# A gather of attention weights in two column halves: an mLSTM with a gated feed-forward layer on one core

## The chip, the cores and the metric

The kernel runs on one core of one Trainium2 chip. The metric is the device time of one launch in microseconds; the lower the better. Of the kernel before there are three timed runs and one profiled execution, which gives the span from the first to the last instruction of the program.

## The reference, cut to what matters

For each of 4 batches and 8 heads, 768 tokens run through a gated recurrence, and its output goes through a gated feed-forward layer:

```
for t in range(S):                                   # S = 768, head size D = 40
    m_new = maximum(f_gate[t] + m, i_gate[t])
    f_stab, i_stab = exp(f_gate[t] + m - m_new), exp(i_gate[t] - m_new)
    C = f_stab * C + i_stab * outer(v[t], k[t])      # 40 x 40 per batch and head
    n = f_stab * n + i_stab * k[t]
    y[t] = sigmoid(o_gate[t]) * (C @ q[t]) / maximum(abs(n @ q[t]), 1)
x = y as 3072 tokens x 320
out = (sigmoid(x @ w_gate) * (x @ w_val)) @ w_out     # 320 -> 1536 -> 320
```

All inputs and the output are float32.

## The kernel before, in words

The recurrence is computed in chunks: 768 tokens are 6 chunks of 128, and with 4 batches that makes 24 *units* (chunk c, batch b), each with 128 tokens and all 8 heads. Within a unit the work is attention-like. The state of the earlier chunks comes in as a separate product.

The stages of a unit, with the names that stand in the profile:

- **a** (`st_a`): q and k are transposed on TensorE (tile `pt`, L357 and L373).
- **b** (`st_b`): the scores of each head, keys on the output's 128 partitions and queries along its columns (tile `s`, L426 in chunks 0 and 1, L434 later), are multiplied on VectorE by the decay matrix (`d`, L427 and L435). The result stays in `d`: 128 keys x 8 heads x 128 queries.
- **c** (`st_c`): the *gather*. For each head one matmul has the 128 x 128 block of `d` as the stationary operand and the head's 128 x 41 values (`v`, with a column of ones for the denominator) as the moving operand: 128 queries x 41 into the PSUM tile `av` (L452). Before it stands the part from the state (`in`, L447). VectorE adds the two (L454) and divides. `st_e` then updates the state (`cs`, L500).
- **d** (`st_d`): the unit's output is transposed (`xt`, L488) into the feed-forward layer's operands `xh` and `xl`.

Around these stages runs the feed-forward layer. `ffn_up` makes, for a tile of 128 hidden columns and 256 or 512 tokens, the gate and value products (`pg`, L532, L534, L537); `ffn_down` multiplies by the output weights (`po`, L554 to L556). Its operands are split in a high and a low part, so each product is made of three matmuls. This layer is most of TensorE's work.

The first two units (0,0) and (0,1) are done in `opening()`, in an order written out by ranks; their gather is a function of its own (L697). Everything after is emitted in the order of a table of positions, and a scheduler then orders each engine's instructions by priority: by default an instruction's place in the program, raised where a piece of code is wrapped in `tc.high_priority(offset=...)`. Stages a to d are wrapped in that with an offset of 1 (`HPO`), weights with 2 (`WPO`). Where instructions of equal standing are ready together, the scheduler mixes them, so a gather's matmuls can stand among those of `pg` or `po`.

Of the kernel before, what the change touches and what calls it, by code (L numbers as in the profile page):

```python
# [67 lines left out]
    },  # L68
    'unpin': [],
}  # L70
GROUPS = ((0, 3), (3, 3), (6, 2))

# [2 lines left out]
def mlstm_then_gated_ffn_kernel(  # L75
# [13 lines left out]
    nc = tc.nc  # L89
    B, H, S, D = q.shape  # L90
    P = 128
# [30 lines left out]
    qt, kt, vt, ot = {}, {}, {}, {}  # L122
# [18 lines left out]
    dm = {}  # L141

    def dm_tile(c, b):
        dm[(c, b)] = big.tile([P, H, L], F32, tag="dmat", name=f"d_{c}_{b}", bufs=3)
        return dm[(c, b)]
# [193 lines left out]
    def bank(c, b, shape, name):  # L339
        return ps_a.tile(shape, F32, tag="pa", name=f"{name}_{c}_{b}")  # L340
# [51 lines left out]
    def stack():  # L392
# [6 lines left out]
        for x, dst, i in ((1, ks, 0), (0, qs, 1)):  # L399
# [4 lines left out]
            nc.sync.dma_start(dst[one].rearrange("p (m g) t -> p m (g t)", m=3).bitcast(F32),  # L404
                              sc[:, 0, :, x, :].rearrange("m d w -> d m w"))

    dlast = {}

    def d_last(u):
# [29 lines left out]
    def st_c(c, b):  # L439
        u = (c, b)  # L440
        nc.scalar.activation(ot[u], ot[u], AF.Tanh, scale=0.5)
        t1 = None
        if c > 0:
            pi = bank(c, b, [P, H, DA], "in")
            for g, (h0, nh) in enumerate(GROUPS):
                r = nh * D
                nc.tensor.matmul(pi[:, h0 : h0 + nh, :], qk[u][:r, g, :], cst[:r, b, g, : nh * DA], start=True, stop=True)  # L447
            t1 = two.tile([P, H, DA], F32, tag="t1", name=f"t1_{c}_{b}")
            nc.vector.tensor_tensor(t1, pi, dec[:, c, b * H : (b + 1) * H].unsqueeze(2).broadcast_to([P, H, DA]), ALU.mult)
        pv = bank(c, b, [P, H, DA], "av")  # L450
        for h in range(H):
            nc.tensor.matmul(pv[:, h, :], dm[u][:, h, :], vt[u][:, h, :], start=True, stop=True)  # L452
        if c > 0:
            nc.vector.tensor_tensor(t1, t1, pv, ALU.add)  # L454
            hs = t1
        else:
            hs = pv
        halfden(u, hs)
        times_den(u)
# [4 lines left out]
    def halfden(u, hs):  # L464
        c, b = u
        den = two.tile([P, H], F32, tag="den", name=f"den_{c}_{b}")
        nc.vector.tensor_scalar(den, hs[:, :, D], -2.0, 2.0, ALU.mult, ALU.max)
        nc.vector.scalar_tensor_tensor(den, hs[:, :, D], 2.0, den, ALU.mult, ALU.max)
        nc.vector.reciprocal(den, den)
        rden[u] = den  # L470
        nc.vector.scalar_tensor_tensor(ot[u], ot[u], 1.0, hs[:, :, :D], ALU.add, ALU.mult)

    def times_den(u):
        c, b = u
        xin[u] = x = two.tile([P, 3 * P], F32, tag="x", name=f"x_{c}_{b}", bufs=1)
        eng = E('ro0' if c == 0 and b < 2 else 'ro')
        eng.tensor_tensor(x[:, :DM].rearrange("p (h d) -> p h d", d=D), ot[u],
                          rden[u].unsqueeze(2).broadcast_to([P, H, D]), ALU.mult)
        E('xd0' if c == 0 and b < 2 else 'xd').tensor_copy(x[:, DM:], x[:, 2 * P : DM])
# [94 lines left out]
    def opening():  # L574
        us = ((0, 0), (0, 1))
# [48 lines left out]
        d = [dm_tile(0, b) for b in range(2)]  # L624
# [5 lines left out]
        pmb, pt, ps, pv, pc, px, sp = {}, {}, {}, {}, {}, {}, {}  # L630
# [5 lines left out]
        def ptile(tag, shape, name):  # L636
            return (ps_a if tag == "pa" else ps_o).tile(shape, F32, tag=tag, name=name)
# [56 lines left out]
        def gather(b):  # L694
            pv[b] = p = ptile(tags["v", b], [P, H, DA], f"av_0_{b}")
            for h in range(H):
                nc.tensor.matmul(p[:, h, :], d[b][:, h, :], vt[us[b]][:, h, :], start=True, stop=True)  # L697

        def ogate(b):
            nc.scalar.activation(ot[us[b]], ot[us[b]], AF.Tanh, scale=0.5)  # L700
# [7 lines left out]
        w = {x: None for x in ((0, 0), (1, 0), (2, 0))}  # L708
# [25 lines left out]
        for b in range(2):  # L734
            for n in range(2):
                op(f"sp{b}{n}", spread, (b, n))
                op(f"ex{b}{n}", expd, (b, n), f"sp{b}{n}")
                op(f"mk{b}{n}", mask, (b, n), f"ex{b}{n}")
            op(f"dl{b}", d_last, (us[b],), f"mk{b}0", f"mk{b}1")
            for g in range(3):  # L740
                op(f"tr{b}{g}", trans, (b, g))
                op(f"cp{b}{g}", copy, (b, g), f"tr{b}{g}")
                op(f"qb{b}{g}", qbd, (b, g), f"cp{b}{g}")
                op(f"sc{b}{g}", score, (b, g), f"qb{b}{g}")
                op(f"ti{b}{g}", times, (b, g), f"sc{b}{g}", f"dl{b}")
            op(f"kw{b}", kweight, (b,), f"dl{b}", *(f"tr{b}{g}" for g in range(3)))
            op(f"og{b}", ogate, (b,))
            op(f"ga{b}", gather, (b,), *(f"ti{b}{g}" for g in range(3)))
            op(f"na{b}", norm_a, (b,), f"ga{b}", f"og{b}")
            op(f"nb{b}", norm_b, (b,), f"na{b}")  # L750
            op(f"xt{b}", st_d, us[b], f"nb{b}")
# [33 lines left out]
    start = [0.0]  # L785
# [9 lines left out]
    for u in range(2, NU):  # L795
        for st in "abcde":
            c, b = divmod(u, B)
# [16 lines left out]
    for u in reversed(range(2, NU)):  # L814
# [5 lines left out]
        n = u + (1 if u == B * (PARAM['V32'] + 1) - 1 else 2)  # L820
# [19 lines left out]
    for u in range(2, NU):  # L840
        c, b = divmod(u, B)
# [18 lines left out]
    def emit(p, kind, kk):  # L860
# [7 lines left out]
        elif kind == "w":  # L868
            with tc.high_priority(offset=PARAM["WPO"]):
                w_next(wseq[kk])  # L870
        elif kind == "g":
            if kk == 0:
                dmat_load(1, 0)
            else:
                gates_of(2, NCH)
        elif kind == "h":
            gate_transpose(ag, at, *((1, 2), (2, NCH))[kk], None)
        elif kind == "k":
            gates_turn(*((1, 2), (2, NCH))[kk])
        elif kind == "e":  # L880
            if last is None:
                dmat(c, b)
            else:
                with tc.issue_after(last.ins):
                    dmat(c, b)
        else:
            with tc.high_priority(offset=PARAM["HPO"]):
                if kind == "a":
                    st_a(c, b)
                elif kind == "b":  # L890
                    st_b(c, b)
                elif kind == "c":
                    st_c(c, b)
                    st_e(c, b)
                    prefetch(c + 1, b)
                else:
                    st_d(c, b)
# [45 lines left out]
```

## Time and profile before

| | |
|---|---|
| Timed runs, median (lowest to highest) | 572.12 us (571.66 to 572.26) |
| Span of the profiled execution | 569.9 us |
| TensorE matmul records, share of the span busy | 96% |
| TensorE weight loads, share of the span busy | 87% |
| VectorE, ScalarE, GpSimd busy | 56%, 41%, 28% |
| Gather, weight loads busy (22 units, L452) | 46.8 us |
| Granted TensorE clock, mean of the span | 0.988 |

The page gives the profiled execution's span and no other time of it; the median of the runs is 2.2 us longer. PE is TensorE's matmuls and PEld its weight loads, which are recorded apart. A float32 matmul in the program shows as two pairs of a weight load and a matmul, so one unit's gather is 16 pairs. Records of neighbouring matmuls overlap, and so their lengths don't add up; the distance from one start to the next does. In a record's shape the first pair of numbers is rows*columns of the stationary operand and the second the shape of what the record names.

### The profile page before, as it was taken

Reading aid. Unit: us, or ns where it says so; the run is one execution under the profiler, and the core shown is the slowest. Engines: PE = TensorE matmul, PEld = TensorE weight load, DVE = VectorE, ACT = ScalarE, POOL = GpSimd, SP = SyncE. Lnnn points to the kernel's source line nnn. Section 1 sums busy time; section 2 is a strip of 40 time slices with the busy share of each in tenths; the row PEclk is TensorE's granted clock in tenths of the full one; section 3 lists DMA queues with packets and bytes.
Section 4 is the critical chain, followed back from the end, with each engine's and each line's share of the span. In section 5 each row is a group of like instructions: output and inputs, shape, how many; then the busy total and the mean of one; then the engine's idle time right before and its main releaser. Section 6 shows DMA issues by size and latency. Waiting matters only on the chain.

```text
span 569.9 us, 9906 instructions
## 1 busy us (share of the span) xinstructions
PE 546.7 (96%) x3587; PEld 497.0 (87%) x3587; DVE 319.5 (56%) x739; ACT 232.2 (41%) x581; POOL 162.2 (28%) x231
## 2 busy tenths in 40 slices
PE   8667999999999999999999999999999999999997
PEld 7565988788899999998888888888888888999996
DVE  5788878895755645555555544545543545432322
ACT  5285657754443442352243241433342332232322
POOL 5567646575420241311322310332210210000000
PEclk9789999999999999999999999999999999999999
DMA  9797747242674947354666544685644824010000
GB/s 197 193 240 185 202 123 192 93 115 54 169 173 119 183 103 182 100 147 125 167 125 156 132 141 129 149 171 124 140 125 134 206 56 121 4 47 2 24 2 23
DMA packets 131641, 72.27 MB, mean 127 GB/s; under 512 B 103113, under 2 KB 120777, under 8 KB 131593
## 3 DMA queue, kind: packets, MB, share of 16 engines
q1 hardware_dynamic: 130504, 71.39, 50.6%
q8 instruction: 28, 0.46, 0.3%
q10 hardware_dynamic: 1088, 0.26, 0.2%
q14 instruction: 21, 0.16, 0.1%
HBM read 56.95 MB, written 14.68 MB: 126 GB/s over the span
## 4 chain that ended last, share of the span: by engine, by line
PE 85%; DVE 7%; ACT 3%; issue 2%; POOL 2%; POOLq 0%; DVEq 0%; ACTq 0%
PE pg L532 34%; PE po L554 7%; PE po L556 7%; PE po L555 7%; PE av L452 6%; PE pg L534 6%; PE pg L537 6%; PE in L447 2%; PE s L434 2%; PE pt L373 2%; PE xt L488 2%; PE cs L500 2%; PE s L426 1%; DVE dc L264 1%; ACT d L226 1%
## 5 line engine op out<-in xcount | busy, mean ns | idle before, releaser
L539 ACT ACTIVATE sg<-pg 128x256 f32<-128x256 f32 (+1 forms) x103 | 48.3, 469 | 174.3 <-PE pg L537 174.2
L540 DVE SCALAR_TENSOR_TENSOR sg<-sg,pg 128x256 f32<-128x256 f32 (+1 forms) x103 | 53.9, 524 | 113.9 <-ACT sg L539 110.6
L532 PE MATMUL pg<-xh,wl 128*128 128x256 f32 (+1 forms) x412 | 111.1, 342 | 1.2 <-POOL wl L304 1.2
L532 PE MATMUL pg<-xh,wh 128*128 128x256 f32 (+1 forms) x412 | 110.9, 343 | 0.4 <-DVE sg L540 0.4
L532 PE MATMUL pg<-xl,wh 128*128 128x256 f32 (+1 forms) x412 | 108.7, 339 | 0.0
L556 PE MATMUL po<-oh,gl 128*128 128x320 f32 x288 | 93.0, 323 | 0.0
L554 PE MATMUL po<-oh,gh 128*128 128x320 f32 x288 | 92.3, 321 | 0.4 <-ACT gh L543 0.4
L555 PE MATMUL po<-ol,gh 128*128 128x320 f32 x288 | 92.4, 321 | 0.0
L544 DVE TENSOR_TENSOR gl<-sg,gh 128x256 fp32r<-128x256 f32 (+1 forms) x103 | 59.6, 579 | 35.5 <-ACT gh L543 34.9
L532 PEld LDWEIGHTS pg<-xh,wl 128*128 128x128 f32 x412 | 70.9, 191 | 8.5 <-POOL wl L304 1.4
L532 PEld LDWEIGHTS pg<-xh,wh 128*128 128x128 f32 x412 | 70.9, 191 | 5.8 <-DVE sg L540 0.6
L532 PEld LDWEIGHTS pg<-xl,wh 128*128 128x128 f32 x412 | 69.3, 190 | 6.6
L543 ACT ACTIVATE gh<-sg 128x256 fp32r<-128x256 f32 (+1 forms) x103 | 51.7, 502 | 47.7 <-DVE sg L540 47.7
L554 PEld LDWEIGHTS po<-oh,gh 128*128 128x128 f32 x288 | 54.5, 189 | 2.0 <-ACT gh L543 0.6
L555 PEld LDWEIGHTS po<-ol,gh 128*128 128x128 f32 x288 | 54.4, 189 | 1.3
L556 PEld LDWEIGHTS po<-oh,gl 128*128 128x128 f32 x288 | 54.2, 188 | 0.5 <-DVE gl L544 0.2
L534 PE MATMUL pg<-xh,w 128*128 128x256 f32 (+1 forms) x206 | 52.9, 332 | 0.7 <-POOL v L139 0.4
L537 PE MATMUL pg<-xl,w 128*128 128x256 f32 (+1 forms) x206 | 53.1, 331 | 0.0
L452 PEld LDWEIGHTS av<-v,d 128*128 128x128 f32 x352 | 46.8, 191 | 2.2 <-DVE d L427 0.6
L452 PE MATMUL av<-v,d 128*128 128x41 f32 x352 | 45.5, 269 | 0.4 <-DVE d L427 0.3
L508 POOL TENSOR_TENSOR cst<-cst,cdec 120x246 f32<-120x246 f32 (+1 forms) x32 | 16.0, 519 | 98.9 <-PE in L447 98.9
L235 POOL TENSOR_SCALAR_AFFINE_SELECT d<-d 128x1024 f32<-128x1024 f32 x22 | 24.2, 1101 | 50.1 <-ACT d L230 46.0
(128 smaller groups left out, 834.5 us busy)
## 6 DMA issues: line engine op xcount, KB each, us to landing
d<-mscr SPq DMA_DIRECT2D x22, 512.0 KB
ks<-scr SPq DMA_DIRECT2D x16, 360.0 KB
qs<-scr SPq DMA_DIRECT2D x16, 360.0 KB
k<-in_k_dram SPq DMA_DIRECT2D x24, 160.0 KB
v<-in_v_dram SPq DMA_DIRECT2D x24, 160.0 KB
o<-in_o_gate_dram SPq DMA_DIRECT2D x24, 160.0 KB
st_o<-in_moe_w_out_dram SPq DMA_DIRECT2D x12, 320.0 KB
out_dram<-ob SPq DMA_DIRECT2D x24, 160.0 KB
```

The lines of the kernel that those rows point to most:

```text
L235: nc.gpsimd.affine_select(out=d, in_=d, pattern=[[0, H], [1, L]], compare_op=ALU.is_ge, fill=0.0, base=0, channel_multiplier=-1)
L452: nc.tensor.matmul(pv[:, h, :], dm[u][:, h, :], vt[u][:, h, :], start=True, stop=True)
L532: nc.tensor.matmul(pg[n], w[n][:, a, fs], x[c][:, a, n0:n1], start=(i + a == 0), stop=False)
L534: nc.tensor.matmul(pg[n], w2[n][:, fs], xh[c][:, 2, n0:n1], start=False, stop=False)
L537: nc.tensor.matmul(pg[n], w2[n][:, fs], xl[c][:, 2, n0:n1], start=False, stop=True)
L539: nc.scalar.activation(sg, pg[0], AF.Tanh, scale=0.5)
L540: nc.vector.scalar_tensor_tensor(sg, sg, 1.0, pg[1], ALU.add, ALU.mult)
L543: last = nc.scalar.activation(gh[u][:, :nt], sg, AF.Copy)
L544: E('gl0' if c == 0 else 'gl').tensor_tensor(gl[u][:, :nt], sg, gh[u][:, :nt].bitcast(F32), ALU.subtract)
L554: nc.tensor.matmul(po[t], g1[:, ts], oh[:, j, :], start=(j == 0), stop=False)
L555: nc.tensor.matmul(po[t], g1[:, ts], ol[:, j, :], start=False, stop=False)
L556: nc.tensor.matmul(po[t], g0[:, ts], oh[:, j, :], start=False, stop=(j == NF - 1))
```

## The change

Each head's gather is made of two matmuls in place of one. The first has the 64 stationary columns of the first 64 queries and writes partitions 0 to 63 of `av`, the second has the other 64 columns and writes partitions 64 to 127. The moving operand is the same 128 x 41 for both. This holds in all 24 units, the opening's too, by a new function `by_columns`. In `st_c` the gather is also wrapped in a priority with an offset of 20. The entries `SC` and `SPO` are not read.

```
+    'AV': 2,
+    'SC': 1,
+    'APO': 20,
+    'SPO': 20,
...
+    def by_columns(dst, lhs, rhs, n):
+        w = P // n
+        for x in range(n):
+            xs = slice(x * w, (x + 1) * w)
+            nc.tensor.matmul(dst[xs], lhs[:, xs], rhs, start=True, stop=True)
...
         pv = bank(c, b, [P, H, DA], "av")
-        for h in range(H):
-            nc.tensor.matmul(pv[:, h, :], dm[u][:, h, :], vt[u][:, h, :], start=True, stop=True)
+        with tc.high_priority(offset=PARAM['APO']):
+            for h in range(H):
+                by_columns(pv[:, h, :], dm[u][:, h, :], vt[u][:, h, :], PARAM['AV'])
...
         def gather(b):
             pv[b] = p = ptile(tags["v", b], [P, H, DA], f"av_0_{b}")
             for h in range(H):
-                nc.tensor.matmul(p[:, h, :], d[b][:, h, :], vt[us[b]][:, h, :], start=True, stop=True)
+                by_columns(p[:, h, :], d[b][:, h, :], vt[us[b]][:, h, :], PARAM['AV'])
```

Line numbers move by 10 or 11: the gather's matmuls all stand at L415 (in `by_columns`), `in` at L457, `cs` at L511, `pg` at L543 and following, `po` at L565 to L567.

How PE's order moves. First, unit (1,0) before, where its gather begins; the numbers in a name are chunk and batch (`av_1_0`), and in `pg0_0_5_0` the half, the chunk, the hidden tile and the first token tile:

```order
L555 MATMUL po3_0_915<-ol_105,gh_0_3_2_1001 128x320
L452 MATMUL av_1_0_1055<-v_1_0_397,d_1_0_451 128x41
L556 MATMUL po3_0_915<-oh_104,gl_0_3_2_1002 128x320
L452 MATMUL av_1_0_1055<-v_1_0_397,d_1_0_451 128x41
L532 MATMUL pg0_0_5_0_1105<-xh_0_343,wh0_98 128x512
L452 MATMUL av_1_0_1055<-v_1_0_397,d_1_0_451 128x41
L532 MATMUL pg0_0_5_0_1105<-xh_0_343,wh0_98 128x512
```

The same place on PE in the changed kernel:

```order
L566 MATMUL po3_0_947<-ol_105,gh_0_3_2_1033 128x320
L415 MATMUL av_1_0_1087<-v_1_0_413,d_1_0_467 64x41 x16
L567 MATMUL po3_0_947<-oh_104,gl_0_3_2_1034 128x320
L543 MATMUL pg0_0_5_0_1145<-xh_0_359,wh0_98 128x512 x2
L543 MATMUL pg0_0_5_0_1145<-xh_0_359,wl0_99 128x512 x2
```

The heads no longer stand apart with a wider matmul between each two; sixteen half-width matmuls stand in one row.

Second, unit (1,1) on PE before, at the end of its part from the state:

```order
L532 MATMUL pg0_0_9_0_1443<-xh_0_343,wh0_98 128x512
L447 MATMUL in_1_1_1383<-cst_106,qk_1_1_1136 128x123
L532 MATMUL pg0_0_9_0_1443<-xh_0_343,wl0_99 128x512
L447 MATMUL in_1_1_1383<-cst_106,qk_1_1_1136 128x82
L532 MATMUL pg0_0_9_0_1443<-xh_0_343,wl0_99 128x512
L452 MATMUL av_1_1_1389<-v_1_1_556,d_1_1_563 128x41
L532 MATMUL pg0_0_9_0_1443<-xl_0_344,wh0_98 128x512
L452 MATMUL av_1_1_1389<-v_1_1_556,d_1_1_563 128x41
```

And in the changed kernel:

```order
L457 MATMUL in_1_1_1423<-cst_106,qk_1_1_1176 128x123
L415 MATMUL av_1_1_1429<-v_1_1_580,d_1_1_587 64x41 x16
L543 MATMUL pg0_0_9_0_1491<-xh_0_359,wh0_98 128x512
L457 MATMUL in_1_1_1423<-cst_106,qk_1_1_1176 128x123
L543 MATMUL pg0_0_9_0_1491<-xh_0_359,wl0_99 128x512
L457 MATMUL in_1_1_1423<-cst_106,qk_1_1_1176 128x82
```

Here the gather has moved ahead of the last two matmuls of `in`, which VectorE reads first, and the matmuls of `pg` follow it whole.

## The prediction

> **What bounds the kernel now.** I read the head of the page first: how busy each engine is, then the chain of work that ended last, then the costliest groups.
>
> ```profile
> span 569.9 us, 9906 instructions
> PE 546.7 (96%) x3587; PEld 497.0 (87%) x3587; DVE 319.5 (56%) x739; ACT 232.2 (41%) x581; POOL 162.2 (28%) x231
> ...
> PE 85%; DVE 7%; ACT 3%; issue 2%; POOL 2%; POOLq 0%; DVEq 0%; ACTq 0%
> PE pg L532 34%; PE po L554 7%; PE po L556 7%; PE po L555 7%; PE av L452 6%; PE pg L534 6%; PE pg L537 6%; PE in L447 2%; PE s L434 2%; PE pt L373 2%; PE xt L488 2%; PE cs L500 2%; PE s L426 1%; DVE dc L264 1%; ACT d L226 1%
> ...
> L452 PEld LDWEIGHTS av<-v,d 128*128 128x128 f32 x352 | 46.8, 191 | 2.2 <-DVE d L427 0.6
> L452 PE MATMUL av<-v,d 128*128 128x41 f32 x352 | 45.5, 269 | 0.4 <-DVE d L427 0.3
> ```
>
> TensorE (PE) is the bound: 85% of the last chain, and the gather (L452) alone 6% of it. Each float32 product shows as two records, each a weight load and a matmul: 22 units x 8 heads x 2 = 352. The other 32 are the opening's (L697). Next, busy time by stretch, from the first unit after the opening to the last up-projection:
>
> ```profile
> 57.00:556.00 499.00, 495.28 (x3291) 452.00 (x3290) 273.15 (x639) 196.71 (x481) 127.47 (x172) 1.00 0.48 121
> ```
>
> Columns: length, then PE, weight loads, DVE, ACT and POOL. PE works 495.28 of 499.00 us at the full granted clock (1.00). PE time saved or added here goes to the end almost one for one, and a shift on another engine costs nothing while PE has this backlog.
>
> What sets a gather's length is in the timeline of the weight loads:
>
> ```profile
> 50.01 1.86 PEld L452 LDWEIGHTS av<-v,d 128*128 128x128 f32 x16 [0.24 <-ACT qk L361]
> 51.79 0.68 PEld L500 LDWEIGHTS cs<-v,k 128*120 128x120 f32 x6
> ```
>
> Sixteen loads from 50.01 until the next line's at 51.79: 1.78 us, 0.111 us each. A load lasts 0.191 us and its matmul 0.269 us, both more than that step, so they overlap, and the step is the weight loads': moving only 41 columns takes less (below, 82 columns step at 0.07). Does a gather hide among wider matmuls? Unit (1,0) answers:
>
> ```profile
> 85.12 0.43 PEld L452 LDWEIGHTS av<-v,d 128*128 128x128 f32 x2
> 85.47 0.19 PEld L532 LDWEIGHTS pg<-xh,wl 128*128 128x128 f32 x1
> 85.58 0.43 PEld L452 LDWEIGHTS av<-v,d 128*128 128x128 f32 x2
> ...
> 308.49 0.63 PE L532 MATMUL pg<-xh,wl 128*128 128x512 f32 x2
> 308.96 0.63 PE L532 MATMUL pg<-xl,wh 128*128 128x512 f32 x2
> ```
>
> One head plus one 512-wide pg takes 0.46 us (85.12 to 85.58). A pg alone takes 0.235 (0.47 for two). The head still costs 0.225, its two loads. So standing together or scattered, a unit's gather costs 1.78 us: 22 x 1.78 = 39.2 us here.
>
> **The change, part by part.** (1) Priority. The order shows each gather as one block (once 15+1), where six units were broken up by wider matmuls and five more had one head apart. By the row above that alone is worth nothing. In some units it also stands a few matmuls earlier; what could be late is DVE's product of scores and weights. DVE stands idle 23.1 us waiting for gathers, and the loads of L452 waited for that product 0.6 us in all (its row above); I take 0.
>
> ```profile
> DVE t L454 <- PE av L452: 23.1, 18, 2.4
> ```
>
> The order of loads, memsets and stores on SP and POOL shifts by a few places with it; DMA share is 0.48 in this stretch, so 0. If that cover were gone, one late transfer would show as a PE wait of a microsecond or so.
>
> (2) Twice as many loads, half as wide: 32 records a unit instead of 16. A narrower load is cheaper, by the two shapes of the state update (window just behind the gather above):
>
> ```profile
> L500 PEld LDWEIGHTS cs<-v,k 128*120 128x120 f32 x4 | 0.5, 184 | 0.0
> L452 PEld LDWEIGHTS av<-v,d 128*128 128x128 f32 x2 | 0.3, 192 | 0.0
> L500 PEld LDWEIGHTS cs<-v,k 128*80 128x80 f32 x2 | 0.3, 150 | 0.1
> ```
>
> (192 - 150) / 48 columns = 0.875 ns a column, so 64 columns fewer take 56 ns off the 111 ns step: 55 to 56 ns for one load.
>
> (3) A narrow tile. The trace has one kind of load that uses only a strip of the array, the gate transposes (32 rows, form 32*128). Around them PE pauses:
>
> ```profile
> 90.20 0.30 PE L500 MATMUL cs<-v,k 128*80 128x82 f32 x2
> 90.43 0.43 PE L195 MATMUL ptg<-ident,gin 32*128 32x32 f32 x4
> 90.79 0.41 PE L554 MATMUL po<-oh,gh 128*128 128x320 f32 x1
> 91.05 0.31 PE L555 MATMUL po<-ol,gh 128*128 128x320 f32 x1
> ...
> 90.43 0.32 PEld L195 LDWEIGHTS ptg<-ident,gin 32*128 32x128 f32 x4
> ...
> L500 PE MATMUL cs<-v,k 128*80 128x82 f32 x2 | 0.3, 234 | 0.0
> ...
> 306.85 0.31 PE L555 MATMUL po<-ol,gh 128*128 128x320 f32 x1
> 307.00 0.31 PE L556 MATMUL po<-oh,gl 128*128 128x320 f32 x1
> ```
>
> The two cs matmuls last 0.234 and end at 90.50, so the second started at 90.27, 0.07 after the first; without a pause the next would start at 90.34. The four ptg loads step at (0.32 - 0.137) / 3 = 0.06. The second po comes 0.26 after the first where 0.15 is usual, so the block really ended at 91.05 - 0.15 = 90.90. That is 0.56 us for 0.24 us of loads: 0.32 us for entering and leaving, the exposed first load of the next line included. (The 0.137 is the mean of these four:)
>
> ```profile
> L195 PEld LDWEIGHTS ptg<-ident,gin 32*128 32x128 f32 x4 | 0.3, 137 | 0.1
> ```
>
> Bounds for a gather in halves: 0 (the 80-column cs shows no pause) to 0.32. A half that must land on output partitions 64 to 127 is a strip of the array, like ptg, so I take 0.32. The Trainium skill ("TensorEngine Tiling (Array Packing)", Key Properties) says that changing the tiling mode drains TensorE; this trace agrees at ptg, with the 0.32 us above.
>
> (4) Whether the two halves load at once. No row shows two loads into different columns. Bounds: 32 steps a unit (one at a time) or 16 (in pairs). The nearest row speaks for one at a time:
>
> ```profile
> 65.44 0.12 PEld L357 LDWEIGHTS pt<-ident,q 128*80 128x80 f32 x1 [0.30 <-DVE cdec L213]
> 65.45 0.23 PEld L532 LDWEIGHTS pg<-xh,wl 128*128 128x128 f32 x1
> 65.62 0.12 PEld L357 LDWEIGHTS pt<-ident,k 128*80 128x80 f32 x1
> 65.72 0.19 PEld L532 LDWEIGHTS pg<-xh,wl 128*128 128x128 f32 x1
> ```
>
> The load issued at 65.45 right behind another takes 0.23 instead of 0.19: it queues. But those two fill the same columns. The halves of a head fill disjoint columns and write disjoint partitions, and the cost per column in (2) is a cost of pushing columns in, which two separate strips need not share. I take pairs, at ptg's 0.06 a step (0.056 by proportion is its lower end): 16 x 0.06 = 0.96, + 0.32 = 1.28 us a unit, 0.50 less than 1.78. The same skill page and section says that different tiles can load and multiply in parallel, which would be this case; no run here shows it yet.
>
> (5) The opening. The last chain and the loads:
>
> ```profile
> 14.25:28.50 14.25, 9.15 (x50) 7.82 (x49) 10.10 (x22) 4.04 (x11) 7.19 (x9) 0.72 0.74 194
> ...
> 20.15 3.41 PE av L697 x16
> 23.56 0.47 PE xt L488 x2
> ...
> 20.15 3.26 PEld L697 LDWEIGHTS av<-v,d 128*128 128x128 f32 x16 [2.79 <-DVE d L689]
> 23.15 0.69 PEld L488 LDWEIGHTS xt<-ident,x 128*128 128x128 f32 x3
> ```
>
> The second opening gather lies on the chain and takes 23.15 - 20.15 = 3.00 us, 1.69 times a usual one, in a stretch whose granted clock is 0.72. Scaled, it saves 0.50 x 1.69 = 0.85. The first is followed by a DVE wait until 20.15, so 0.
>
> Sum: 22 x 0.50 + 0.85 = 11.85 us off a span of 569.9. The median of the runs, 572.12, is 2.2 us over that span (start and end around it), and I leave those as they are: 572.1 - 11.9 = **560.3 us**. With 0.056 steps a unit is 1.22, giving 559.
>
> **The rivals.** *One load at a time* (slower). The mechanism is at the weight loads of L452: if halves queue like the rows at 65.45, a unit takes 32 x 0.056 = 1.79 + 0.32 = 2.11, or 2.24 at 0.06. That is 0.33 to 0.46 more in 22 units and 0.6 to 0.8 in the opening: +7.9 to +10.9, 580 to 583 us. It decides once a pair of halves takes longer than (1.78 - 0.32) / 16 = 0.091 us. For it: every close pair of loads in this trace queues. Against it: none of them are to different columns. The Trainium skill ("TensorE: Matmul & The Clock Gate", The mechanism) says a weight load overlaps matmuls in flight only where the row group differs, and here both halves use all rows; but L452's loads, all of one row group, already start while matmuls of 0.269 us are in flight, so the trace does not bear that rule out as it stands.
>
> *Half overlap.* If records keep their order (two loads of one half, then two of the other), only neighbouring loads of different halves may pair: three steps a head, 24 x 0.06 = 1.44 + 0.32 = 1.76. That is 0.02 less: 571.6, no change.
>
> *No pause.* If the halves cost no entry and exit (as the 80-column cs), with pairs: 0.96 a unit, 0.82 x 22 + 1.4 = 19.4 off: 552.7.
>
> **How the numbers follow.** Pairs with a pause 0.59 (own range 555 to 566), no pause 0.04, half overlap 0.10, one at a time 0.27. This kernel's measurement tells 0.2%, 1.1 us, from no change. Half overlap spreads around zero by some 2 us, as the pause may be 0.1 us off per unit: 0.04 of it faster, 0.04 same, 0.02 slower. Faster 0.59 + 0.04 + 0.04 = 0.67, same 0.04, slower 0.27 + 0.02 = 0.29. The range goes from 554, just above the case without pause, to 582, which takes in about half of one at a time; some 0.17 is left out.
>
> **What would show it.** Right: the gather's loads in the timeline at 32 a unit, with two starts per 0.06 us and some 1.0 us from first to last; PE busy time in the stretch down by some 10 us; before the first and behind the last a gap of 0.1 to 0.2 us; 5 to 6% of the chain in L452 (now L415) becoming 4 to 5%. Wrong: loads stepping at 0.055 to 0.065 each (one at a time), a block of 1.4 us (half overlap), or a gather that starts without a gap. Were waits of the gather for DVE to reach 0.2 us a unit, part (1) would be wrong by 5 us.

## The result, and the profile after

The changed kernel takes 577.71 us (median of 4 runs, 574.92 to 578.26) beside 571.89 us for the kernel before in the same session: ratio 1.0102, 95% interval [1.0073, 1.0131]. It is slower by 1.0%; 560.3 us had been forecast. Among the experiments below, one execution of e10 (the profiled one, 733 us at a granted clock of 0.65 throughout) and one of e4 (625.8 us) are left out of the ratios. The changed kernel's profiled execution took 577.27 us, with this page (head, the chain of waits by engine and by line) and, from the groups kept apart by shape, these rows of the gather:

```profile
span 575.6 us, 10660 instructions
PE 541.6 (94%) x3971; PEld 484.0 (84%) x3971; DVE 329.9 (57%) x739; ACT 231.5 (40%) x581; POOL 159.5 (28%) x231
...
PE 79%; DVE 8%; POOL 4%; ACT 4%; issue 3%; DMA 2%; SPq 0%; POOLq 0%; DVEq 0%; ACTq 0%
PE pg L543 32%; PE po L567 7%; PE po L565 6%; PE po L566 6%; PE pg L548 5%; PE pg L545 5%; PE av L415 4%; PE in L457 3%; PE s L444 2%; PE pt L377 2%; PE cs L511 2%; PE xt L499 1%; DVE dc L273 1%; PE s L436 1%; PE mb L654 1%
...
L415 PE MATMUL av<-v,d 128*64 128x41 f32 x768 | 29.1, 237 | 3.4 <-DVE d L700 2.4 <-POOL d L233 0.9
L415 PEld LDWEIGHTS av<-v,d 128*64 128x64 f32 x768 | 26.0, 144 | 7.8 <-DVE d L700 3.2 <-POOL d L233 1.0 <-issue 0.7
```

The gather did become cheaper: its share of the chain fell from 6% to 4%, and its loads (the opening's are now among them) are busy for 26.0 us. But PE is 79% of the chain instead of 85%; other engines have taken the rest. The timeline of the weight loads shows one gather:

```profile
174.48 0.52 PEld L457 LDWEIGHTS in<-cst,qk 120*128 120x128 f32 x4
175.12 1.01 PEld L415 LDWEIGHTS av<-v,d 128*64 128x64 f32 x32
176.18 0.30 PEld L457 LDWEIGHTS in<-cst,qk 80*128 80x128 f32 x2
```

Thirty-two loads, of 0.144 us each by the group's mean, from 175.12 to 176.13: sixteen pairs step at (1.01 - 0.144) / 15 = 0.058 us. The next line's load comes 1.06 us after the gather's first, where it came after 1.78. The pause is there too: 0.12 us from the end of `in`'s loads (175.00) to the gather's first.

Where time was lost instead shows first in the busy time by stretch. These two rows are the same work in the kernel before and in the changed one, from the first `po` of chunk 0 to the first of chunk 1 (columns as in the prediction's stretch row). Before:

```profile
41.63:152.80 111.17, 105.29 (x658) 91.19 (x657) 89.90 (x200) 67.44 (x180) 68.40 (x80) 1.00 0.54 141
```

After:

```profile
41.27:159.00 117.73, 106.66 (x754) 90.27 (x753) 95.41 (x200) 67.33 (x179) 67.44 (x80) 0.96 0.51 134
```

This stretch alone became 6.6 us longer. The granted clock fell from 1.00 to 0.96, and VectorE (DVE) has the same 200 instructions but is busy with them for 95.41 instead of 89.90 us. How much of this is the new order's doing is for the experiments to tell.

To compare whole executions I add up three things from the records. *Idle*: every time of over 60 ns in which neither a weight load nor a matmul ran. *Clock*: half of the time in which a weight load or a matmul ran while the granted clock was 0.5 ("half-clock windows" below). *Work*: what is left of the span. The differences are of the unrounded numbers.

```
kernel (profiled)                     span    work    idle   clock
before                                569.9   546.6   18.0    5.2
changed                               575.6   536.9   28.3   10.4
changed - before                       +5.7    -9.7  +10.3   +5.2
```

TensorE's work fell by 9.7 us, most of the forecast 11.85. Waits and half-clock windows took back 15.4.

### The profile page after: what moved, and what is told of

Same layout as the page of the kernel before. It is cut to its first block, busy times and chain, and to the rows that moved or that the text cites. A ratio compares the mean times of both kernels' runs of the same rounds, so it can differ in the third digit from the quotient of the medians.

```text
span 575.6 us, 10660 instructions
## 1 busy us (share of the span) xinstructions
PE 541.6 (94%) x3971; PEld 484.0 (84%) x3971; DVE 329.9 (57%) x739; ACT 231.5 (40%) x581; POOL 159.5 (28%) x231
## 4 chain that ended last, share of the span: by engine, by line
PE 79%; DVE 8%; POOL 4%; ACT 4%; issue 3%; DMA 2%; SPq 0%; POOLq 0%; DVEq 0%; ACTq 0%
PE pg L543 32%; PE po L567 7%; PE po L565 6%; PE po L566 6%; PE pg L548 5%; PE pg L545 5%; PE av L415 4%; PE in L457 3%; PE s L444 2%; PE pt L377 2%; PE cs L511 2%; PE xt L499 1%; DVE dc L273 1%; PE s L436 1%; PE mb L654 1%
## 5 line engine op out<-in xcount | busy, mean ns | idle before, releaser
L543 PE MATMUL pg<-xh,wl 128*128 128x256 f32 (+1 forms) x412 | 109.5, 341 | 1.2 <-POOL wl L308 1.2
L543 PE MATMUL pg<-xh,wh 128*128 128x256 f32 (+1 forms) x412 | 110.0, 341 | 0.3
L543 PE MATMUL pg<-xl,wh 128*128 128x256 f32 (+1 forms) x412 | 108.4, 338 | 0.0
L567 PE MATMUL po<-oh,gl 128*128 128x320 f32 x288 | 92.8, 322 | 0.3 <-DVE gl L555 0.2
L565 PE MATMUL po<-oh,gh 128*128 128x320 f32 x288 | 92.2, 320 | 0.5 <-ACT gh L554 0.4
L555 DVE TENSOR_TENSOR gl<-sg,gh 128x256 fp32r<-128x256 f32 (+1 forms) x103 | 61.0, 592 | 38.5 <-ACT gh L554 37.9
L543 PEld LDWEIGHTS pg<-xh,wl 128*128 128x128 f32 x412 | 70.3, 191 | 8.9 <-POOL wl L308 1.4
L543 PEld LDWEIGHTS pg<-xl,wh 128*128 128x128 f32 x412 | 69.9, 190 | 7.5
L543 PEld LDWEIGHTS pg<-xh,wh 128*128 128x128 f32 x412 | 70.7, 191 | 6.2 <-ACT sg L550 0.8
L565 PEld LDWEIGHTS po<-oh,gh 128*128 128x128 f32 x288 | 55.0, 191 | 2.7 <-ACT gh L554 1.0
L545 PE MATMUL pg<-xh,w 128*128 128x256 f32 (+1 forms) x206 | 54.4, 336 | 1.5 <-POOL w L312 1.1
L567 PEld LDWEIGHTS po<-oh,gl 128*128 128x128 f32 x288 | 54.5, 189 | 1.5 <-DVE gl L555 1.3
L548 PE MATMUL pg<-xl,w 128*128 128x256 f32 (+1 forms) x206 | 54.2, 339 | 0.0
L545 PEld LDWEIGHTS pg<-xh,w 128*128 128x128 f32 x206 | 35.3, 190 | 5.2 <-POOL w L312 1.3
L233 POOL TENSOR_TENSOR d<-at,d 128x1024 f32<-128x1024 f32 x16 | 30.9, 1931 | 29.1 <-DMA d<-mscr 24.9
```

What stands on the lines that cost most here:

```text
L233: E(arg).tensor_tensor(d, a, d, ALU.subtract)
L543: nc.tensor.matmul(pg[n], w[n][:, a, fs], x[c][:, a, n0:n1], start=(i + a == 0), stop=False)
L545: nc.tensor.matmul(pg[n], w2[n][:, fs], xh[c][:, 2, n0:n1], start=False, stop=False)
L548: nc.tensor.matmul(pg[n], w2[n][:, fs], xl[c][:, 2, n0:n1], start=False, stop=True)
L555: E('gl0' if c == 0 else 'gl').tensor_tensor(gl[u][:, :nt], sg, gh[u][:, :nt].bitcast(F32), ALU.subtract)
L565: nc.tensor.matmul(po[t], g1[:, ts], oh[:, j, :], start=(j == 0), stop=False)
```

## The experiments

Theory A: the halves save what was forecast, and the changed order costs more than that. Theory B: a gather in halves itself costs time around it, wherever it stands. To part them, kernels were built whose order on all engines is laid down by a table, with one edge from each instruction to the next (no wait is added by it):

```
+    def in_order(table):
...
+            for a, b in zip(seq, seq[1:]):
...
+                tc.add_manual_dep(b, a.name, mybir.DependencyInfo(mybir.DependencyClass.NoSync, ...))
+    in_order(ORDER)
```

A gather is one block in such a table, at the place of its last head. "Old order" is that of the kernel before, "new order" that of the changed one. Line numbers in these kernels are about 90 higher. The ratios (to the kernel before, in the same session) are what is compared, since the kernel before itself moved between 571.9 and 573.3 us; 0.1% is 0.57 us.

### Halves and order, apart (e1, e2, e13)

e1, halves in the old order; the table holds the kernel before's order of all five engines:

```
     'AV': 2,
...
+ORDER = {
+    'PE': (
...
+    ),
...
+}
```

> Halves as in the change, but every engine keeps the order of the kernel before; each gather stands as one block where its last head stood. Theory A (the order is what costs: the gather itself saves 11 to 12 us, and the new order makes TensorE wait and lose clock for some 17): 560 us, 557 to 564, with no new TensorE waits over 1 us after 60 us. Theory B (halves cost time around them, by pauses and lost clock, wherever they stand): 575 us or more.

e2, whole heads in the new order, the changed kernel with its own order in the table and

```
-    'AV': 2,
+    'AV': 1,
```

> Whole heads (one matmul each, 128 columns) as before, in the changed kernel's order on every engine. Theory A: the waits of the new order come without the saving, 580 to 590 us, with TensorE waiting 1 to 2 us at the gate transposes, the state update and the output transposes as in the changed kernel. Theory B: 572 us, as before.

e13, whole heads in the old order, each gather in one block (e1 with `'AV': 1`):

> Whole heads (128 stationary columns) in the old order of all engines, each gather as one block where its last head stood: the halves in the old order (564.9 us) with the halves undone. If the halves are what saves there and a block by itself costs and gives nothing: 571 to 573 us, as the kernel before (572.1). If the blocks save: 565 to 569. If blocks of whole heads cost by letting VectorE wait for the gather's end: over 574.

Measured, with the changed kernel as the fourth corner:

```
              old order                              new order
whole heads   e13 573.17 us, 0.9997 [0.9969, 1.0025]   e2 582.67 us, 1.0160 [1.0087, 1.0232]
halves        e1  564.91 us, 0.9855 [0.9782, 0.9929]   changed 577.71 us, 1.0102 [1.0073, 1.0131]
```

Halves save 1.4% (8.1 us) in the old order and 0.6% (3.3 us) in the new. The new order costs 1.6% (9.3 us) with whole heads and 2.5% (14.1 us) with halves. The intervals of the halves and of the order are clear of each other in every pair but one: e2 and the changed kernel overlap, so the 0.6% is not clear of noise. Theory A holds in the main (e1 came 0.9 us above its range) and B, with 575 us or more for e1, falls. A block by itself costs nothing (e13), as part (1) had it for whole heads.

The profiled executions of the four corners, added up as above (one execution each; e1's, at 568.28 us, is the slowest of its four and 3.4 us over their median):

```
kernel (profiled)                     span    work    idle   clock
e13, whole heads, old order           570.2   546.9   18.1    5.2
e1, halves, old order                 566.6   533.2   23.3   10.1
e2, whole heads, new order            581.4   549.1   25.3    7.0
changed: halves, new order            575.6   536.9   28.3   10.4
```

In the old order the halves take 13.7 us off the work, and 5.1 us of idle time and 4.9 us of lost clock come back. The new order adds 7.2 us idle, 2.2 work and 1.8 clock to whole heads, and 5.0, 3.7 and 0.3 to halves. So the clock that the changed kernel loses is hardly the order's: e1, without that order, loses as much.

The length of the stretch shown above (first `po` of chunk 0 to first `po` of chunk 1), and of all that follows it:

```
                                 stretch   behind it
e13, whole heads, old order       111.2      417.4
e1, halves, old order             116.4      408.9
e2, whole heads, new order        115.6      425.2
changed: halves, new order        117.7      416.6
```

The larger part of what the order costs lies behind the stretch: 7.9 us with whole heads and 7.7 with halves, of which 4.4 and 3.9 are idle time and 3.5 and 3.8 work, with no half-clock window there. Why the same matmuls make more work in the new order isn't shown; it is spread over `pg`, `po` and `in`.

### Each part of the change alone, with the scheduler's own order (e3, e4)

e3, only the priority (`'AV': 1`):

> The priority of 20 without the halves; the scheduler makes its own order. Theory A if the priority makes the bad order: 575 to 588 us. Theory A if only the doubled count of matmuls makes it: 572 us. Theory B: 572 us.

e4, only the halves:

```
-        with tc.high_priority(offset=PARAM['APO']):
-            for h in range(H):
-                by_columns(pv[:, h, :], dm[u][:, h, :], vt[u][:, h, :], PARAM['AV'])
+        for h in range(H):
+            by_columns(pv[:, h, :], dm[u][:, h, :], vt[u][:, h, :], PARAM['AV'])
```

> The halves without the raised priority; the scheduler mixes the halves with wider matmuls in some units, so that there are more changes between narrow and wide matmuls. Theory A: what the order gives, 560 to 575 us. Theory B with a pause of 0.3 us at each change: over 580 us.

Measured: e3 576.24 us, 1.0049 [1.0012, 1.0086]; e4 617.9 us, 1.0738 [1.0639, 1.0838]. With whole heads the priority gives another order than the changed kernel's, and that one costs 0.5%. Halves without it are far slower, out of theory A's range and over theory B's 580 us, because the scheduler mixes them with wide matmuls and each change between the two costs a pause. The timeline of the loads in e4:

```profile
84.43 0.19 PEld L415 LDWEIGHTS av<-v,d 128*64 128x64 f32 x2 [0.24 <-issue]
84.67 0.19 PEld L542 LDWEIGHTS pg<-xh,wl 128*128 128x128 f32 x1
85.10 0.19 PEld L415 LDWEIGHTS av<-v,d 128*64 128x64 f32 x2 [0.24 <-issue]
```

A half (two records) and one `pg` take 0.67 us (84.43 to 85.10). The `pg` is 0.235 by the prediction's rows, and two narrow loads are 2 x 0.056. That leaves 0.32 us for going from wide to narrow and back: the pause of part (3). e4 has 136 narrow stretches where e1 has 24; 112 x 0.32 = 36 us of the 41.2 by which its work is larger (574.4 against 533.2). So in the scheduler's own order the raised priority is what keeps the halves together, and it is also what brings the costly order.

### Do two halves load at once? (e8, e12)

e8, old order, the loops exchanged, so that neighbouring loads go to the same columns:

```
         for x in range(n):
             xs = slice(x * w, (x + 1) * w)
+            for h in range(H):
-            nc.tensor.matmul(dst[xs], lhs[:, xs], rhs, start=True, stop=True)
+                nc.tensor.matmul(dst[xs, h, :], lhs[:, h, xs], rhs[:, h, :], start=True, stop=True)
```

> Halves in the old order with the loops exchanged: in each gather the first halves of all eight heads, then the second halves, so that neighbouring loads go to the same columns. If two loads overlap only when their columns differ, they queue: 32 steps of 0.058 us instead of 16, 0.93 us more in each of 22 units and some 1.6 more in the opening: 564.9 + 22 = 587 us. If narrow loads are as quick in any order: 565 us.

e12, old order, `'AV': 4`, four matmuls of 32 columns a head:

> Old order, each head's gather in four matmuls of 32 stationary columns. If four strips load at once, a set of four takes 0.03 us (half of a pair's 0.058) or at least the 0.035 us that 41 moving columns take by half of the 0.07 of 82: 16 x 0.035 + 0.34 = 0.90 us a unit instead of 1.27, 8 us less in 22 units: 556 to 558 us. If only two load at once, 32 x 0.03 as before: 564 to 566 us. If 128 instructions a unit are issued too slowly: over 567 us.

Measured: e8 574.38 us, 1.0028 [1.0007, 1.0049]; e12 561.94 us, 0.9808 [0.9774, 0.9841]. The gather's loads and the line behind them, e8:

```profile
169.85 1.73 PEld L507 LDWEIGHTS av<-v,d 128*64 128x64 f32 x32
171.63 0.19 PEld L634 LDWEIGHTS pg<-xh,wl 128*128 128x128 f32 x1
```

e12:

```profile
171.92 0.69 PEld L505 LDWEIGHTS av<-v,d 128*32 128x32 f32 x64
172.67 0.19 PEld L633 LDWEIGHTS pg<-xh,wl 128*128 128x128 f32 x1
```

The same 32 half-width loads take 1.78 us to the next line in e8 and 1.06 us in the changed kernel and in e1. Between e1 and e8 nothing but their sequence differs, so loads to different columns overlap and loads to the same columns queue. Quarters take 0.75 us with twice as many records: four overlap. By the loads' mean of 0.114 us for 32 columns a set of four steps at (0.69 - 0.114) / 15 = 0.038 us, above the 0.03 of the proportion and near the 0.035 taken as the floor.

The times moved less than the work in both (587 us had been expected of e8 if loads to the same columns queue, 556 to 558 us of e12 if four overlap):

```
            work     time by the ratios
e1 -> e8    +17.7    +1.73%, +9.9 us
e1 -> e12    -8.1    -0.47%, -2.7 us
e13 -> e1   -13.7    -1.42%, -8.1 us
```

Idle time is 23.3 us in e1, 17.9 in e8 and 25.9 in e12: the shorter TensorE's work, the longer it waits for the others. A microsecond of TensorE's work is worth 0.3 to 0.6 us here; the 0.3, from e12, is rough, as the intervals of e1 and e12 overlap.

### Where the order's cost lies (e5, e6, e7, e9, e10, e14)

The longest new wait after the first 60 us is in unit (1,1). In the changed kernel the state update's first matmul waits 2.02 us for VectorE's `t`, and a half-clock window follows. Timeline of VectorE, of that matmul and of two instructions of GpSimd (POOL):

```profile
118.48 1.40 DVE L273 SCALAR_TENSOR_TENSOR dc<-st,dc 128x256 int32<-128x256 int32 x1
119.56 0.78 POOL L519 TENSOR_TENSOR cst<-cst,cdec 120x246 f32<-120x246 f32 x1
119.80 0.72 DVE L268 TENSOR_SCALAR dc<-dc 128x320 f32<-128x320 f32 x1
120.47 0.72 POOL L312 TENSOR_TENSOR w<-dc,w 64x256 fp32r<-64x256 f32 x1
120.55 0.82 DVE L269 TENSOR_SCALAR dc<-dc 128x320 int32<-128x320 int32 x1
121.30 0.48 DVE L459 TENSOR_TENSOR t<-in,dec 128x328 f32<-128x328 f32 x1
...
121.83 0.47 PE L511 MATMUL cs<-v,k 128*120 128x123 f32 x2 [2.02 <-DVE t L459]
```

The busy time by stretch, changed kernel, just behind it (the column before the last two is the granted clock):

```profile
122.70:126.10 3.40, 3.40 (x14) 3.03 (x13) 3.30 (x7) 2.59 (x8) 2.72 (x2) 0.51 0.02 5
```

The same work in the kernel before:

```profile
116.91 1.39 DVE L269 SCALAR_TENSOR_TENSOR dc<-st,dc 128x256 int32<-128x256 int32 x1
118.22 0.49 DVE L449 TENSOR_TENSOR t<-in,dec 128x328 f32<-128x328 f32 x1
118.63 0.31 DVE L264 TENSOR_SCALAR dc<-dc 128x320 f32<-128x320 f32 x1
118.97 0.33 DVE L265 TENSOR_SCALAR dc<-dc 128x320 int32<-128x320 int32 x1
...
119.99 0.37 PE L500 MATMUL cs<-v,k 128*120 128x123 f32 x2
```

VectorE now does two steps of decoding a weight (`dc`) ahead of `t`, and they take 0.72 and 0.82 instead of 0.31 and 0.33 us; each ends 0.18 us after a GpSimd instruction that was running when it began. To get from the one order to the other, at least 91 of VectorE's 739 instructions have to be moved, and 194 of TensorE's 3,035 outside the gather. I first blamed the gather's own place, as it had moved ahead of the last two matmuls of `in`:

e5, new order, that one block four places later on TensorE (behind `in`):

> The changed kernel with one block moved: unit (1,1)'s gather stands four places later on TensorE, behind the last two matmuls of its part from the state; the rest of the order is the changed kernel's (577.7 us). If the order's cost is made of single waits, this takes away the one at 119.8 us (2.0 us) and the half-clock window behind it (3.4 us at half speed, 1.7 us): 574.0 us, and no half-clock window near 122.7 us. If the cost is spread, or the wait only moves to the next user of the same PSUM bank: 576.5 to 578.5 us.

e6, new order, 17 gathers later on TensorE:

> The changed kernel with 17 of its 22 scheduled gathers moved back on TensorE (13 to the place they had before the change, four as far towards it as the PSUM tiles' order allows); everything else on all engines in the changed kernel's order. If the early place of the gathers is what costs, this should come near the halves in the old order (564.9 us): 565 to 570 us. If it is the rest of the order that the priority has reshuffled (other matmuls, and the other engines): 575 to 579 us.

e7, old order, gathers forward to the changed kernel's places (its table moves 16, not the 17 of the text):

> Halves in the old order (564.9 us when run before) with 17 gathers moved forward on TensorE to the place that they have in the changed kernel; everything else on all engines as in the old order. If the early place of the gathers is what costs: 571 to 578 us. If it is the reshuffled rest: 564 to 567 us.

Measured: e5 576.49 us, 1.0073 [1.0043, 1.0103]; e6 574.54 us, 1.0038 [1.0012, 1.0063]; e7 569.73 us, 0.9930 [0.9901, 0.9958]. In e5 the wait is still there:

```profile
121.87 0.47 PE L600 MATMUL cs<-v,k 128*120 128x123 f32 x2 [2.04 <-DVE t L548]
```

So my reading of that wait was wrong. e6 and e7 came out between their two ranges: the gathers' places cost 0.6 to 0.75% (e6 against the changed kernel, e7 against e1), a quarter to a third of the order's 2.5%. The second is not clear of noise, as the intervals of e7 and e1 overlap. The rest had to lie in the other matmuls' places or with the other engines.

e9, new order, two moves on VectorE alone (unit (1,1); L288 is the copy `at`, L617 the state update `cst`, L548 `t`, L355 and L356 `dc`):

```
- L617 cst, L617 cst, L360 dc, L288 at      + L288 at, L617 cst, L617 cst, L360 dc
- L355 dc, L356 dc, L548 t                  + L548 t, L355 dc, L356 dc
```

> The changed kernel with two moves on VectorE alone: in unit (1,1) the sum t (L459) stands again ahead of two steps of a weight's decoding (L268, L269) instead of behind them, and the copy of the transposed gates (L201) stands ahead of the two state updates (L528) and one decoding step. TensorE and all else keep the changed kernel's order (577.7 us). If the cost of the order lies in what VectorE does first, the waits of TensorE at 91.3 us (1.9 us) and 119.8 us (2.0 us) fall to under 0.5 us each and the half-clock window at 122.7 us (3.4 us, worth 1.7) may go too: 571 to 574.5 us. If those waits only move to the next product: 576 to 578.5 us.

Measured: 574.62 us, 1.0034 [1.0005, 1.0063], 0.7% better than the changed kernel. The matmul that waited 2.02 us, in e9's timeline, and the stretch at 122.7:

```profile
120.92 0.49 DVE L548 TENSOR_TENSOR t<-in,dec 128x328 f32<-128x328 f32 x1
...
121.46 0.47 PE L600 MATMUL cs<-v,k 128*120 128x123 f32 x2 [0.50 <-DVE t L548]
```

```profile
122.70:126.10 3.40, 3.40 (x22) 3.12 (x21) 3.30 (x7) 2.35 (x8) 3.24 (x4) 1.00 0.21 78
```

Wait and half-clock window are gone there. The other move failed: the wait for `at` (1.86 us at 91.3 in the changed kernel) became one of 1.64 us for `qk` on ScalarE at 91.7. And behind that wait, at 95.4 us, e9's trace has a half-clock window of 3.4 us that the changed kernel's has not, so in all e9 lost as much to the clock (10.5 us against 10.4). Idle time fell by 0.9 us and work by 0.6; the profiled executions are 1.4 us apart, less than the 0.7% of the timed runs.

The stretched `dc` steps point to a mechanism of their own. Later in the changed kernel, where from `t` on VectorE's order is as before, its timeline beside GpSimd's (POOL) and TensorE's shows:

```profile
325.31 2.35 DVE L555 TENSOR_TENSOR gl<-sg,gh 128x512 fp32r<-128x512 f32 x1
328.58 1.86 DVE L479 SCALAR_TENSOR_TENSOR den<-t,den 128x8 f32<-128x8 f32 x1
...
325.21 1.90 POOL L233 TENSOR_TENSOR d<-at,d 128x1024 f32<-128x1024 f32 x1
328.37 2.06 POOL L233 TENSOR_TENSOR d<-at,d 128x1024 f32<-128x1024 f32 x1 [1.21 <-DVE den L478]
...
328.12 0.55 PE L499 MATMUL xt<-ident,x 128*128 128x128 f32 x3 [1.30 <-DVE t L465]
331.63 0.41 PE L499 MATMUL xt<-ident,x 128*128 128x128 f32 x2 [1.63 <-DVE x L488]
```

`den` needs 0.16 us and took 1.86: it ended at 330.44, as GpSimd's subtraction did (330.43). `gl` needs 0.68 and ended at 327.66, 0.55 after the subtraction's end at 327.11. Both are held until GpSimd is done, and TensorE then waits 1.30 and 1.63 us. In the kernel before the subtraction ran from 320.76 to 322.65, and VectorE's `gl` was through at 320.6. Over the changed kernel, grouped by whether a GpSimd TENSOR_TENSOR ran at the time: `t` (L465, which reads the gather in PSUM) takes 0.49 us alone and 0.49 us beside one (3 times); `den` (L479, after chunk 0) 0.16 and 1.39 (5 times); `x` (L488) 0.49 and 1.32 (3 times). The Trainium skill ("GPSIMD Engine Reference", Specifications) says that GpSimd shares its way to SBUF with VectorE, and that VectorE's instructions with two SBUF inputs, or in a two-port mode, contend with it. The trace agrees for `gl`, `den` and `x`, with these numbers.

e10, new order, that subtraction in four:

```
-            E(arg).tensor_tensor(d, a, d, ALU.subtract)
+            n = 4
+            ins = [E(arg).tensor_tensor(d[:, x : x + H // n, :], a[:, x : x + H // n, :], d[:, x : x + H // n, :], ALU.subtract).ins
+                   for x in range(0, H, H // n)]
```

> The changed kernel with GpSimd's decay subtraction (L233, 1.9 us for all eight heads) in four instructions of two heads, in the same place of GpSimd's order; from chunk 1 on. In the changed kernel's trace VectorE's gl took 2.35 us instead of 0.68 and den 1.86 instead of 0.16 while such a subtraction ran, and TensorE then waited 1.30 us (326.8) and 1.60 us (330.0). If VectorE is held until GpSimd's instruction ends, it is held at most 0.5 us now, the two waits fall below 0.6 us each: 573.5 to 576 us. If the stretch has another cause: 577 to 579 us, with the waits as they were.

e14, the moves of e6 and of e9 and this split, together:

> The changed kernel with the three repairs together: 17 gathers later on TensorE, the two moves on VectorE, GpSimd's subtraction in four. Alone they gave 3.2, 3.1 and 3.4 us. If they are separate parts of the order's cost: 577.7 - 9.7 = 568 us, within 3 us of the halves in the old order. If they repair the same waits: 571 to 575 us.

Measured: e10 574.27 us, 1.0029 [1.0005, 1.0053]; e14 571.74 us, 0.9959 [0.9937, 0.9982]. What e10's two waits became is not shown. Alone the three repairs gave 0.64, 0.68 and 0.73%; together 1.43% of 2.05%: mostly separate parts. (In microseconds e14 stands in the range set for repairs of the same waits, but in that session the kernel before took 573.25 us; by the ratio e14 is at 569.5.) Each repair is clear of the changed kernel, but none alone is clear of e5, which has a table too and stands 0.3% below it; e14 is clear of all of them. Of the 2.47% between the changed kernel and e1 that leaves 1.04%, 5.9 us. In e14's trace three waits stand where e1 has 0.6, none and 0.5 us: 1.31 us (`pt`, at 91.6), 1.71 (`pt`, 211.8) and this one:

```profile
326.86 0.33 PE L593 MATMUL xt<-ident,x 128*128 128x128 f32 x1 [2.11 <-POOL x L584]
...
324.30 2.33 POOL L323 TENSOR_TENSOR d<-at,d 128x256 f32<-128x256 f32 x4 [1.76 <-DMA d<-mscr]
326.57 0.24 POOL L584 COPY x<-x 128x64 f32<-128x64 f32 x1
```

The last comes from GpSimd's order: in the new order its copy of `x` stands behind the subtraction, whole or in four (e6, with the subtraction whole, waits 1.67 us for the same copy); in the old order the copy comes first (e1, at 324.67, with the subtraction at 325.37). No repair moved it back.

The three are 4.0 us more than e1's. The two profiled executions are 3.8 us apart: e14 has 3.0 us more idle and 2.5 more work, and lost 1.7 less to the clock. The repairs acted on the stretch up to 153 us, which is 112.0 us long in e14 (117.7 in the changed kernel); behind it e14 takes 417.2 us, 8.3 more than e1. What else makes up the 5.9 us between the timed runs stays open, and it is to be looked for there.

### Versions that beat both (e11, e15)

e11 is e1 with the subtraction in four, e15 is e12 with it.

> Halves in the old order (564.9 us) with the same split of GpSimd's subtraction. In that run TensorE has fewer waits that end on such a stretch (0.5 us at 324.2, 1.0 us at 408.2): 563 to 565 us if VectorE is held by GpSimd, 565 to 567 us if not.

> Old order, quarters of 32 columns (561.9 us) and GpSimd's subtraction in four (which gave 1.8 us with halves). If both add: 560 us. If less weight loading now only makes TensorE wait longer for VectorE: 561 to 563 us.

Measured: e11 563.07 us, 0.9833 [0.9798, 0.9869]; e15 560.13 us, 0.9762 [0.9723, 0.9801]. Both stand lower than their bases by the size expected, though the intervals overlap (0.9855 and 0.9808), so the split's own gain in the old order isn't shown. e11's trace shows why it is small, in the timelines of VectorE and GpSimd:

```profile
315.65 1.57 DVE L573 TENSOR_SCALAR den<-t 128x8 f32<-128x8 f32 x1
...
314.82 2.32 POOL L324 TENSOR_TENSOR d<-at,d 128x256 f32<-128x256 f32 x4
```

The four pieces follow each other at once, and in this case VectorE got in only behind the last of them (317.14), not after one piece as expected. Quarters in the old order are the best version: 2.4% faster than the kernel before with the split, 1.9% without.

## Why the prediction was wrong

**Part (1), the priority at 0, is the step that failed.** "By the row above that alone is worth nothing" is true of a block of whole heads (e13, 0.9997) and was taken for the whole of what the priority does. The order it makes costs 1.6% with whole heads and 2.5% with halves. I looked for lateness at one place, the gather's own wait for VectorE's product. That place stayed quiet: of the 3.4 us that L415's matmuls waited, 2.4 are the opening's (L700), 0.9 one wait for GpSimd (L233), and 0.1 is left. The waits came at `cs`, `pt` and `xt`, which part (1) did not look at: e9 shows that the one at `cs` comes from VectorE's order, and the traces put those at `xt` beside GpSimd's instructions. The slack on which I took 0, VectorE's wait for gathers, has shrunk to a third; the waits of the changed kernel have, in place of 23.1 us:

```profile
DVE t L465 <- PE av L415: 7.4, 9, 1.7
```

The sign that I set ("waits of the gather for DVE") was therefore the wrong one to watch. Some 1% of the 2.5% was not taken away by any repair, and its cause is traced only in part.

**"A shift on another engine costs nothing"** failed with it. The stretch row from 57 to 556 us averaged over stages. From 41.6 to 152.8 us PE is busy for 105.29 of 111.17 us in the kernel before, beside a VectorE busy for 89.90; from 152.8 to 565 for 410.35 of 412.20. The first has little slack on either engine. But the new order costs most behind it (7.7 to 7.9 us), where PE had been busy all the time: a busy PE did not mean a backlog that hides a late input.

The 6.6 us by which the first stretch lengthened, on the other hand, are for the most part not the order's: e1, in the old order, has 5.3 of them (next row). e8, where the gathers are long again (the row after), has none. e1:

```profile
41.23:157.67 116.44, 107.03 (x754) 90.28 (x753) 94.77 (x202) 67.50 (x180) 68.89 (x79) 0.96 0.52 137
```

e8:

```profile
41.70:152.91 111.21, 105.88 (x754) 90.72 (x753) 90.47 (x200) 67.00 (x179) 67.70 (x79) 1.00 0.55 142
```

In e1 the work of this stretch is 3.3 us less than in the kernel before, but 3.6 us of idle time and 5.1 us of lost clock are added, and VectorE is busy longer. Its gain all comes later: 408.9 us behind the stretch against 417.1 before. There the changed kernel gains nothing (416.6). How much e1 loses in the stretch differs between executions: e11, with the same halves and order but GpSimd's subtraction in four, needs 111.8 us for it. **"Almost one for one"** was too high: 0.3 to 0.6 by the three pairs above, the rest being taken by idle time and the clock.

**The clock** was not in the sum. Between 50 and 570 us of the changed kernel, windows at half clock begin at 54.5, 122.7 and 150.1 us; the kernel before has none there. The one at 122.7 went when the wait ahead of it went (e9), but e9 has another at 95.4. Not each such wait brings one: none follows the 1.86 us at 91.3 us in the changed kernel, and one follows the 1.64 us at 91.7 us in e9. e1 has windows at 54.4 and 146.5 us and is faster than the kernel before all the same. What decides it is open.

**Parts (2) to (4)** were right: a step of 0.058 us for most single loads in e8, where 0.055 to 0.056 was forecast, and the same 0.058 for a pair in the changed kernel, a pause of 0.32 (e4), pairs (e8 against e1). TensorE's work fell by 9.7 us (before to changed) to 13.7 us (e13 to e1), around the 11.85. The rival with one load at a time, at 580 to 583 us, would have come out nearest to the time, and for the wrong reason; that the measured time lies below the upper end of the range, 582, is luck, since the range reaches so far only for that rival's sake. The Trainium skill's statement that different tiles load in parallel ("TensorEngine Tiling (Array Packing)", Key Properties) is now shown by a run, at 1.06 against 1.78 us for the same loads.

**Part (5)** was right as a block and less at the end. The changed kernel's opening:

```profile
20.13 1.79 PE L415 MATMUL av<-v,d 128*64 128x41 f32 x32 [2.37 <-DVE d L700]
22.26 0.90 PE L499 MATMUL xt<-ident,x 128*128 128x128 f32 x3 [0.34 <-POOL x L488]
26.57 0.90 PE L499 MATMUL xt<-ident,x 128*128 128x128 f32 x3 [3.41 <-POOL x L488]
```

The second gather's successor begins 2.13 us after it instead of 3.00 (by the weight loads, as in the prediction), though some of that is a new wait for GpSimd (0.34 by the matmuls). The next `xt` stood at 27.17 before: of the 0.85 us, 0.60 arrive.

## What to carry to other kernels

A priority is not an edit to one engine. Before it is valued at nothing, compare the order on every engine, and ask of each moved instruction who waits for it. That the bound engine is busy all the time does not show that it has work in hand while an input is late.

Where a matmul with few moving columns is bound by loading its stationary operand, cut that operand into column strips and issue the strips of one operand in turn; keep all of them together, since each change between narrow and wide costs 0.32 us here.

When the busiest engine's work is cut, expect less than that back: find out which waits grow, and whether the clock falls.

## What the runs showed of the hardware

- Loads of 64 columns that go to different halves of the columns overlap: sixteen pairs step at 0.058 us, whereas 32 loads, half by half, take 1.78 us to the next line, as 16 of 128 columns do. Four strips of 32 columns overlap as well, at 0.038 us a set.
- VectorE instructions with two SBUF inputs that started while a GpSimd TENSOR_TENSOR ran were held until about its end: 1.86 us for one that needs 0.16. One that reads PSUM beside SBUF was not (0.49 us both ways). Cutting GpSimd's instruction in four did not always let VectorE in between: one instruction took 1.57 us, through the rest of the four.
- A wait of 2.0 us in a busy stretch was followed within a microsecond by 3.4 us at a granted clock of 0.5 (122.7 us), and taking away most of the wait took that window away (e9). In e9 another of 3.4 us came at 95.4 us, behind a wait of 1.64 us, where the changed kernel has none behind 1.86 us.
